# Attention and two MLP layers on one core: four copies per head for six, P x V with one group per column half, another order of work

## The chip, the cores and the metric

The kernel runs on one core of one Trainium2 chip. The metric is device microseconds of one execution. Five engines run side by side, each through its own instructions in order: PE (TensorE, matmul), DVE (VectorE), ACT (ScalarE), POOL (GpSimd) and SP (SyncE, which issues nearly all DMA transfers).

## The reference

Two batches of eight heads, sequence 768, head dimension 64, float32. Each query and each key gets a six-bit bucket from the signs of its projection; a query attends only to keys of its own bucket. The attention output goes through two MLP layers of width 512, 2048, 512.

```python
q_bits = (np.einsum('bhsd,dk->bhsk', q, proj) > 0)      # k_bits the same
mask = q_bucket[:, :, :, None] == k_bucket[:, :, None, :]
scores = np.where(mask, 0.125 * np.matmul(q, k.transpose(0, 1, 3, 2)), -1e9)
attn = softmax(scores)
x = np.matmul(attn, v)                   # to (1536, 512)
h = x @ moe_w_in; x = (P(h) / Q(h)) @ moe_w_out          # rational function
h = x @ moe2_w_in; out = (h * clip(h + 3, 0, 6) / 6) @ moe2_w_out
```

## The kernel before

**Precision.** Products whose operands are split are done as sums of products of a high part (rounded to the matmul format fp32r) and a low part (the rest). A high part is written by ACT or POOL, a low part by DVE or POOL.

**Attention.** The work is 16 heads of three groups, 48 groups in all; a group is 256 query rows in two row blocks of 128. For each head, PE transposes Q and K together (`tp_mm`, L220), ACT copies the result out (`tp_full`), `tp_hi` (TH) and `tp_lo` (TL) make the tiles `th` and `tl`: rows 0 to 63 are Q, rows 64 to 127 are K. The score matmul needs Q and K parts on other partitions, in four tiles: `q1` (q high over q low), `k1` (k high twice), `q2` (q high, then 12 rows of bits) and `k2` (k low, then 12 rows of bits). DMA copies on SP fill them: `spread_hi` (SPH, L244) issues four copies out of `th`, `spread_lo` (SPL, L250) two out of `tl`, `spread_bits` (SB, L270) four small ones out of the bucket bits. Each of the four tiles has two buffers, so the copies of a head wait until the score matmuls of the head two before it are done.

For each group: scores (`s_mm`, S: L342 with `q1` and `k1`, L345 with `q2` and `k2`), row maximum on DVE (L349), exponential on ACT, normalisation on POOL (L370), transposes of P on PE (`p_mm`, L378), copies of them out of PSUM on ACT or DVE (`p_copy`, L388), then P x V (`v_mm`, L396). P x V is done for two groups at a time. Within a group the two row blocks go to the two column halves of the array, 128 columns each, with one PSUM tile `o` per group; `v_out` empties each tile by two copies, the first on ACT, the second on DVE (L409) behind it. PSUM tiles with the tag `T` (transposes, bits, P, `o`) share four buffers.

**Weights.** In the same time the weights of the MLP are loaded (`conv_load`, raw, L102) and split by ACT, DVE and POOL (`conv_a`, `conv_r`, `conv_s`, L119, `conv_add`, `conv_hi`, `conv_lo`). 13 of the 32 tiles of the first layer are ranked by a list `CVS`, the others by their due step and `AHEAD`.

**Layers.** 96 steps follow (2 layers, 3 token blocks, 16 hidden blocks), each of 24 matmuls of 512 columns: 12 into `h` (`in_mm`, L448) and 12 into `acc` (`out_mm`, L516), with the function between them on ACT, DVE and POOL.

**Order.** Everything after `start()` is a list of tasks with engines, rank, dependencies and the buffers they take. `ordered()` walks a model of the engines: whenever an engine is free it takes the ready task of lowest rank. Durations are in `W`, delays to a dependent in `W_LAG` and `LAG`, ranks come from `OFF`, `W_SLOT` per group, `CVS` and `AHEAD`. The instructions are emitted in that order and every engine keeps it, whatever the real durations are. SP is modelled as one engine that is held for a whole transfer.

Of the kernel before, what the change touches and what calls it, by code (L numbers as in the profile page):

```python
# [24 lines left out]
KP = D + 2 * NB  # L25
# [3 lines left out]
CVS = (1, 6, 11, 13, 14, 20, 25, 28, 28, 34, 36, 48, 55)  # L29
RING = {"raw": 3, "cvd": 3, "t1": 2, "t2": 3, "t3": 2, "t4": 1, "gh": 2, "gl": 2}  # L30

W = {"S": 0.70, "M": 0.87, "E": 0.89, "NV": 0.53, "A": 0.28, "N": 0.97, "P": 0.44, "H": 0.485, "H_D": 0.60, "V": 2.85, "OC": 0.23,
     "VA": 0.25, "XH": 0.35, "XL": 0.71, "TP": 0.33, "TF": 0.47, "TH": 0.74, "TH_P": 0.98, "TL": 0.86, "TL_P": 1.95, "Z": 0.85, "ZB": 0.59, 
# [3 lines left out]
     "ld": 2.0, "LQ": 1.6, "LV": 0.9, "SPH": 3.1, "SPL": 1.6, "SB": 1.3, "cf": 1.0}  # L37
W_LAG = {"PE": 0.25, "DVE": 0.13, "ACT": 0.16, "POOL": 0.09, "SP": 2.5, "NONE": 0.0}
LAG = {"A": 0.30, "E": 0.26, "ld": 3.0, "LQ": 2.8}
TLP = 0  # L40
W_SLOT = 5.091

OFF = {"S": -7.496, "rr": -1.217, "M": 7.071, "E": -43.196, "NV": -36.242, "A": 8.173, "N": -5.796, "P": 12.751, "H": 2.136, "V": -12.378, "OC":
       -30.545, "VA": -24.667, "XH": 7.594, "XL": 6.524, "TP": 14.245, "Z": 9.031, "c": -4.166, "SPH": 8.232, "SPL": -22.569, "SB": -11.64, "LQ": -19.047,
       "LV": -42.52, "ld": -12.092, "cf": 7.164}
AHEAD = 0.2557
# [4 lines left out]
def body(tc, q, k, v, proj, moe_w_in, moe_w_out, moe_a, moe_b, moe2_w_in, moe2_w_out, out):  # L51
# [89 lines left out]
    nat, tf, hl, lr, live = {}, {}, {}, {}, {}  # L141
# [15 lines left out]

    zfill = ate.tile([128, 512], F32R, name="zfill")
# [53 lines left out]
    thr = cpool.tile([128, 4], F32, name="thr")  # L212
    zw = ate.tile([128, 32], F32, name="zw")
# [14 lines left out]
    def tp_hi(hd, eng):  # L228
        hl[hd] = tuple(ate.tile([128, S], F32R, name=f"t{x}", tag=f"t{x}{hd % 2}") for x in "hl")
        if eng == "POOL":  # L230
            nc.gpsimd.tensor_scalar(out=hl[hd][0], in0=tf[hd], scalar1=1.0, scalar2=0.0, op0=ALU.mult, op1=ALU.add)
        else:
            act(hl[hd][0], tf[hd])
# [5 lines left out]
    def spread_hi(hd):  # L239
        th = f(hl[hd][0])  # L240
        t = lr[hd] = [ate.tile([128, S], F32R, name=x, tag=x, bufs=2) for x in ("q1", "q2", "k1", "k2")]
        q1, q2, k1, k2 = (f(x) for x in t)
        for dst, src in ((q1[0:64], th[0:64]), (k1[0:64], th[64:128]), (k1[64:128], th[64:128]), (q2[0:64], th[0:64])):
            nc.sync.dma_start(out=dst, in_=src)  # L244

    def spread_lo(hd):
        tl = f(hl[hd][1])
        q1, q2, k1, k2 = (f(x) for x in lr[hd])
        for dst, src in ((q1[64:128], tl[0:64]), (k2[0:64], tl[64:128])):
            nc.sync.dma_start(out=dst, in_=src)  # L250
# [15 lines left out]
    def spread_bits(hd):  # L266
        for i in range(2):
            for n in range(2):
                o = 64 * (hd % 2) + 32 * n + 2 * NB * i
                nc.sync.dma_start(out=f(lr[hd][2 * i + 1])[64:KP, n * 384:(n + 1) * 384], in_=f(live["bt"])[o:o + 2 * NB])  # L270

# [12 lines left out]
    def start():  # L284

        th, tl = hl[0] = tuple(ate.tile([128, S], F32R, name=f"t{x}", tag=f"t{x}0") for x in "hl")
        q1, q2, k1, k2 = lr[0] = [ate.tile([128, S], F32R, name=x, tag=x, bufs=2) for x in ("q1", "q2", "k1", "k2")]

        for n in range(2):
            tp_mm(0, n)  # L290
            c = slice(n * 384, (n + 1) * 384)
            ps = live.pop(("tp", 0, n))
            act(th[:, c], ps, scale=qsc)
            stt(tl[:, c], ps, qsc, f(th)[:, c], ALU.mult, ALU.subtract)
            for dst, t in ((k1[0:64], th), (k1[64:128], th), (k2[0:64], tl)):
                nc.gpsimd.tensor_scalar(out=dst[:, c], in0=f(t)[64:128, c], scalar1=1.0, scalar2=0.0, op0=ALU.mult, op1=ALU.add)
        load_qk(2)
        load_v(0)
        load_v(1)
# [4 lines left out]
        act(q2[0:64], th[0:64])  # L304
# [9 lines left out]
        nc.vector.tensor_copy(out=k2[64:KP], in_=f(bt)[32:32 + 2 * NB])  # L314
        nc.vector.tensor_copy(out=q2[64:KP], in_=f(bt)[0:2 * NB])
# [19 lines left out]
    def s_mm(g, rr):  # L335
        hd, rg = divmod(g, 3)
        q1, q2, k1, k2 = lr[hd]
        r = 2 * rg + rr
        rs = slice(r * 128, (r + 1) * 128)
        ps = sps[(g, rr)] = psc.tile([128, 2, 512], F32, name="s", tag="S", bufs=2)  # L340
        for n in range(2):
            nc.tensor.matmul(out=ps[:, n, 0:384], lhsT=q1[:, rs], rhs=k1[:, n * 384:(n + 1) * 384],  # L342
                             start=True, stop=False)
        for n in range(2):
            nc.tensor.matmul(out=ps[:, n, 0:384], lhsT=q2[0:KP, rs], rhs=k2[0:KP, n * 384:(n + 1) * 384],  # L345
                             start=False, stop=True)
# [43 lines left out]
    def v_mm(g):  # L390
        vs = nat[("v", g // 3)]
        o = live[("o", g)] = psum.tile([128, 128], F32, name="o", tag="T", bufs=4)
        for kt in range(R):
            pt = pts[(g, kt // 2)]
            for rr in range(2):
                nc.tensor.matmul(out=o[64 * rr:64 * rr + 64], lhsT=vs[:, kt], rhs=pt[:, kt % 2, rr * 128:rr * 128 + 128],  # L396
                                 start=(kt == 0), stop=(kt == R - 1))
        for i in range(3):
            pts.pop((g, i))

    def v_out(g, rr):
        main = slice(64 * (g // 3 % 2), 64 * (g // 3 % 2) + 64)
        if rr == 0 and (g // 3) % 2 == 0:
            xts[g % 3] = atl.tile([128, 256], F32, name="xt", tag=f"xt{g % 3}")
        dst, src = xts[g % 3][main, rr * 128:rr * 128 + 128], live[("o", g)][64 * rr:64 * rr + 64]
        if rr == 0:
            act(dst, src)
        else:
            nc.vector.tensor_copy(out=dst, in_=src)  # L409
            live.pop(("o", g))  # L410
# [128 lines left out]
    def add(name, engines, rank, deps, fn, port=(), earliest=0.0, takes=(), frees=()):  # L539


        work[name] = (engines if isinstance(engines, dict) else dict([engines]), rank, [d for d in deps if d in work],
                      fn, port, earliest, takes, frees)

    def plan_attention():
# [3 lines left out]
        def pair(pr):  # L549
# [3 lines left out]
            for hd in heads:  # L553
                if hd > 2:
                    add(("LQ", hd), ("SP", W["LQ"]), (g0 - 9 + 2 * (hd % 2)) * T + OFF["LQ"], [("TP", hd - 2, 1)], lambda e, hd=hd: load_qk(hd))
                for n in range(2):
                    r = (g0 - 9 + 2 * (hd % 2) + n) * T + OFF["TP"]
# [5 lines left out]
                add(("TH", hd), {"ACT": W["TH"], "POOL": W["TH_P"]}, r + 1.2, [("TF", hd, 0), ("TF", hd, 1), ("SPH", hd - 2), ("SPL", hd - 2)],  # L563
                    lambda e, hd=hd: tp_hi(hd, e), pool)
                add(("TL", hd), {"DVE": W["TL"], "POOL": W["TL_P"]}, r + 1.8, [("TH", hd)], lambda e, hd=hd: tp_lo(hd, e), ("POOL", "DVE"))
            r = (g0 - 5) * T + OFF["Z"]
# [4 lines left out]
            for hd in heads:  # L571
                r = (g0 - 4 + 3 * (hd % 2)) * T
                old = [("S", 3 * (hd - 2) + 2, 1)]
                add(("SPH", hd), ("SP", W["SPH"]), r + OFF["SPH"], [("TH", hd)] + old, lambda e, hd=hd: spread_hi(hd))
                add(("SPL", hd), ("SP", W["SPL"]), r + OFF["SPL"], [("TL", hd), ("SPH", hd)], lambda e, hd=hd: spread_lo(hd))
                add(("SB", hd), ("SP", W["SB"]), r + OFF["SB"], [("ZB", pr), ("SPH", hd)], lambda e, hd=hd: spread_bits(hd))

        def vals(hd):
            if hd > 1:
                add(("LV", hd), ("SP", W["LV"]), (3 * hd - 3) * T + OFF["LV"], [("V", 3 * hd - 4 + (hd % 2 == 0))], lambda e: load_v(hd))  # L580

        def group(g):
            hd = g // 3
            b = g * T
            odd, last = hd % 2, g >= NG - 5
            for rr in range(2):
                add(("S", g, rr), ("PE", W["S"]), b + OFF["S"] + OFF["rr"] * rr, [("SB", hd), ("SPL", hd)], lambda e, rr=rr: s_mm(g, rr), takes=("S",),
                    earliest=1.0)
                add(("M", g, rr), ("DVE", W["M"]), b + OFF["M"] + OFF["rr"] * rr, [("S", g, rr), ("N", g - 4, 1)], lambda e, rr=rr: s_max(g, rr))
                add(("E", g, rr), ("ACT", W["E"]), b + OFF["E"] + OFF["rr"] * rr, [("M", g, rr)], lambda e, rr=rr: s_exp(g, rr), takes=("p",),  # L590
# [10 lines left out]
            if g % 2:  # L601
                two = (g - 1, g)
                add(("V", g), ("PE", W["V"]), b + OFF["V"], [("H", x, i) for x in two for i in range(3)] + [("LV", hd), ("LV", (g - 1) // 3)],
                    lambda e: [v_mm(x) for x in two], takes=("T", "T"), frees=tuple(("H", x, i) for x in two for i in range(3)))
                for x in two:
                    add(("OC", x), ("ACT", W["OC"]), b + OFF["OC"], [("V", g), ("XL", x - 3)], lambda e, x=x: v_out(x, 0))
                    add(("VA", x), ("DVE", W["VA"]), b + OFF["VA"], [("OC", x), ("XL", x - 3)], lambda e, x=x: v_out(x, 1),
                        frees=(("V", g),) if x == g else ())
                    if x // 3 % 2:
                        add(("XH", x), {"POOL": W["XH"], "ACT": W["XH"]} if last else ("POOL", W["XH"]), b + OFF["XH"], [("VA", x)],  # L610
# [131 lines left out]
    def ordered():  # L742
# [14 lines left out]
        free, port, held, out, now = {}, 0.0, None, [], 0.0  # L757
# [99 lines left out]
```

## Time and profile before

| | |
|---|---|
| Time, median of 3 runs | 773.3 us (771.25 to 944.34) |
| Time of the profiled execution | 774.28 us |
| Its span, first to last instruction | 772.5 us |
| PE busy | 756.2 us (98%) |
| DVE, ACT, POOL busy | 537.3, 478.8, 384.0 us (70, 62, 50%) |
| DMA | 65.76 MB |

A profile row names a line, an engine, an operation, output<-input, and a count. Busy time of PE counts overlapping matmuls once, and ends of matmuls are modelled; start times are the surer reading. An fp32 matmul that is no transpose shows as two records. In the profile text, "idle before" names what released the engine.

### The profile page before, as it was taken

To read this page: it belongs to the slowest core of one execution; us is meant where nothing else is said; L and a number is where in the kernel's file an instruction comes from. 1 tells how busy PE (TensorE), PEld (TensorE's weight loads), DVE (VectorE), ACT (ScalarE), POOL (GpSimd) and SP (SyncE) were. 2 spreads that over 40 slices of the span, in tenths; PEclk is the share of its full clock that TensorE was granted. 3 is DMA by queue.
4 is the path that set the end of the run, shared out by engine and by line. 5 is a ranking of instruction groups with operands and counts; after the bars stand their busy time and mean duration, and the time that the engine had idled before them with its cause. 6 is when DMAs were issued, how large, how long until landed. Compare 5 with 4: busy or idle time off the path is not lost.

```text
span 772.5 us, 12661 instructions
## 1 busy us (share of the span) xinstructions
PE 756.2 (98%) x4603; PEld 641.1 (83%) x4603; DVE 537.3 (70%) x905; ACT 478.8 (62%) x890; POOL 384.0 (50%) x446
## 2 busy tenths in 40 slices
PE   7989999999999999999999999999999999999998
PEld 6879989888898888888888888888888888888886
DVE  6867989878788999999889999987522322232222
ACT  6878888788567788876558889877422222222221
POOL 6878999979678667722224667877400000000000
PEclk9999999999999999999999999999999999999999
DMA  7785766675331133300002033345100100010001
GB/s 192 190 225 152 181 186 174 155 191 160 104 87 39 71 110 110 109 1 1 0 1 82 5 105 120 113 142 178 49 1 1 55 1 1 0 55 1 0 1 54
DMA packets 47485, 65.76 MB, mean 85 GB/s; under 512 B 29168, under 2 KB 31936, under 8 KB 47424
## 3 DMA queue, kind: packets, MB, share of 16 engines
q1 hardware_dynamic: 46640, 64.76, 29.5%
q8 instruction: 36, 0.59, 0.3%
q10 hardware_dynamic: 784, 0.20, 0.1%
q14 instruction: 25, 0.20, 0.1%
HBM read 43.00 MB, written 3.15 MB: 60 GB/s over the span
## 4 chain that ended last, share of the span: by engine, by line
PE 84%; DMA 6%; ACT 3%; DVE 3%; POOL 1%; issue 1%; SPq 1%; ACTq 0%; POOLq 0%; DVEq 0%
PE acc L516 34%; PE h L448 33%; PE o L396 5%; PE tt L378 5%; PE s L342 3%; PE s L345 3%; DMA raw<-in_moe_w_out_dram 1%; ACT p L55 1%; DMA raw<-in_moe_w_in_dram 1%; DMA k<-th 1%; DMA nv<-in_v_dram 1%; DVE stat L349 1%; SPq L270 1%; DVE t L58 1%; POOL p L370 1%
## 5 line engine op out<-in xcount | busy, mean ns | idle before, releaser
L55 ACT ACTIVATE t<-h,cbias 128x512 f32<-128x512 f32 x48 | 33.0, 689 | 122.9 <-PE h L448 122.9
L505 POOL TENSOR_TENSOR gl<-t,gh 128x512 fp32r<-128x512 f32 x48 | 62.9, 1310 | 92.6 <-ACT gh L55 89.1
L370 POOL TENSOR_SCALAR p<-p,stat 128x768 f32<-128x768 f32 x96 | 100.5, 1055 | 15.5 <-DVE stat L366 7.3
L58 DVE SCALAR_TENSOR_TENSOR t<-t,h 128x512 f32<-128x512 f32 x48 | 33.1, 689 | 108.0 <-ACT t L55 108.0
L123 POOL TENSOR_TENSOR cvd<-cvd,raw 128x512 int32<-128x512 int32 x64 | 87.8, 1376 | 36.0 <-DVE cvd L119 20.7
L349 DVE TENSOR_REDUCE stat<-s 128x1 f32<-128x768 f32 x96 | 88.4, 949 | 8.2 <-PE s L345 7.5
L55 ACT ACTIVATE p<-s,stat 128x768 f32<-128x768 f32 x96 | 85.9, 903 | 12.3 <-DVE stat L349 10.4
L55 ACT ACTIVATE gh<-t 128x512 fp32r<-128x512 f32 x96 | 60.6, 632 | 50.7 <-PE acc L516 42.0
L378 PE MATMUL tt<-ident,p 128*128 128x128 f32 x576 | 71.8, 276 | 2.3 <-ACT pt L55 2.3
L505 DVE TENSOR_TENSOR gl<-t,gh 128x512 fp32r<-128x512 f32 x48 | 37.5, 782 | 51.0 <-PE acc L516 47.5
L58 DVE SCALAR_TENSOR_TENSOR t<-t,coef,h 128x512 f32<-128x512 f32 x96 | 71.4, 744 | 1.7
L378 PEld LDWEIGHTS tt<-ident,p 128*128 128x128 f32 x576 | 66.1, 142 | 6.6 <-ACT pt L55 1.7
L58 DVE SCALAR_TENSOR_TENSOR t<-t,r 128x512 f32<-128x512 f32 x96 | 65.9, 687 | 5.6 <-ACT r L55 2.6
L396 PE MATMUL o<-pt,nv 128*64 128x128 f32 x1152 | 68.6, 275 | 1.0 <-ACT tf L55 1.0
L396 PEld LDWEIGHTS o<-pt,nv 128*64 128x64 f32 x1152 | 62.4, 137 | 8.0 <-issue 4.3
L342 PE MATMUL s<-k,q 128*128 128x384 f32 x192 | 56.0, 372 | 3.2 <-ACT p L55 3.1
L388 DVE COPY pt<-tt 128x512 f32<-128x512 f32 x81 | 51.6, 682 | 4.6 <-PE tt L378 4.0
L516 PE MATMUL acc<-gh,wo_0h 128*128 128x512 f32 x192 | 54.2, 389 | 0.0
L516 PE MATMUL acc<-gh,wo_0l 128*128 128x512 f32 x192 | 54.2, 389 | 0.0
L516 PE MATMUL acc<-gl,wo_0h 128*128 128x512 f32 x192 | 54.2, 389 | 0.0
L516 PE MATMUL acc<-wo_0h,gh 128*128 128x512 f32 x192 | 54.2, 389 | 0.0
L516 PE MATMUL acc<-wo_0l,gh 128*128 128x512 f32 x192 | 54.2, 389 | 0.0
(139 smaller groups left out, 1809.0 us busy)
## 6 DMA issues: line engine op xcount, KB each, us to landing
raw<-in_moe_w_in_dram SPq DMA_DIRECT2D x32, 512.0 KB
raw<-in_moe_w_out_dram SPq DMA_DIRECT2D x32, 512.0 KB
q<-th SPq DMA_DIRECT2D x30, 192.0 KB
k<-th SPq DMA_DIRECT2D x30, 192.0 KB
nqk<-in_q_dram SPq DMA_DIRECT2D x16, 192.0 KB
nv<-in_v_dram SPq DMA_DIRECT2D x16, 192.0 KB
out_dram<-o SPq DMA_DIRECT2D x12, 256.0 KB
nqk<-in_k_dram SPq DMA_DIRECT2D x15, 192.0 KB
```

The source lines that it names most:

```text
L55: nc.scalar.activation(out=out, in_=in_, func=func, **kw)
L58: nc.vector.scalar_tensor_tensor(out=out, in0=in0, scalar=scalar, in1=in1, op0=op0, op1=op1)
L123: nc.gpsimd.tensor_tensor(out=d.bitcast(I32), in0=d.bitcast(I32), in1=raw[:, :, 0], op=ALU.add)
L342: nc.tensor.matmul(out=ps[:, n, 0:384], lhsT=q1[:, rs], rhs=k1[:, n * 384:(n + 1) * 384], start=True, stop=False)
L349: nc.vector.tensor_reduce(out=stats[g % 4][:, rr, 0:1], in_=sps[(g, rr)][:, :, 0:384], axis=AX.XY, op=ALU.max, negate=True)
L370: nc.gpsimd.tensor_scalar(out=pt, in0=pt, scalar1=st[:, rr, 4:5], scalar2=st[:, rr, 5:6], op0=ALU.mult, op1=ALU.add)
L378: nc.tensor.transpose(ps[:, kt, rr], ptile[(g, rr)][:, c:c + 128], ident)
L388: nc.vector.tensor_copy(out=pt, in_=live.pop(("p", g, i)))
L396: nc.tensor.matmul(out=o[64 * rr:64 * rr + 64], lhsT=vs[:, kt], rhs=pt[:, kt % 2, rr * 128:rr * 128 + 128], start=(kt == 0), stop=(kt == R ...
L448: nc.tensor.matmul(out=ps, lhsT=w[:, ws], rhs=x[:, cols(m)], start=(n == 0), stop=(n == 3 * KD - 1))
L505: (nc.gpsimd if eng == "POOL" else nc.vector).tensor_tensor(out=e["gl"], in0=e["2"], in1=f(e["gh"]), op=ALU.subtract)
L516: nc.tensor.matmul(out=acc["o"][i], lhsT=lhsT, rhs=rhs, start=(t == 0 and n == 0), stop=(t == NF - 1 and n == 2))
```

## The change

**K parts in place.** `th`, `tl`, `q1`, `q2` get three buffers each; `k1` and `k2` no longer exist except for head 0. `spread_q` (SPH) copies q high to `q1[0:64]` and to `q2[64:128]`; `spread_k` (SPK) copies k high over the q half of `th`, so that `th` is what `k1` was; `spread_lo` copies q low to `q1[64:128]`; k low stays in `tl[64:128]`, and the bits go over the first 12 rows of `tl` and of `q2`. Rows 12 to 63 of `q2` are zeroed once. So SPK waits for SPH and TL, and the bits of a head wait for its SPH and SPL. The second score matmul contracts over 128 rows instead of 76.

**P x V.** One PSUM tile of 128x256 for the pair: group g-1 in the lower column half, group g in the upper one, 256 columns per matmul. `v_out` is one copy per group, on ACT or DVE.

**Order.** Each DMA task becomes an issue on SP and a transfer on a modelled engine "DMA". `W`, lags, ranks, `CVS`, `W_SLOT` and `AHEAD` have new values; the first two V loads leave `start()` and become ranked tasks. `FREE0` sets when engines are first free.

```diff
-CVS = (1, 6, 11, 13, 14, 20, 25, 28, 28, 34, 36, 48, 55)
+CVS = (-4, 12, 12, 12, 15, 21, 27, 28, 30, 33, 35, 54, 57)
...
-     "ld": 2.0, "LQ": 1.6, "LV": 0.9, "SPH": 3.1, "SPL": 1.6, "SB": 1.3, "cf": 1.0}
-W_LAG = {"PE": 0.25, "DVE": 0.13, "ACT": 0.16, "POOL": 0.09, "SP": 2.5, "NONE": 0.0}
+     "ld": 1.65, "LQ": 1.75, "LV": 0.6, "SPH": 1.55, "SPK": 0.78, "SPL": 0.78, "SB": 0.25, "cf": 0.1}
+ISSUE = {"ld": (0.4, 0), "LQ": (0.65, 0.65), "LV": (0.65, 0), "SPH": (0.6, 0.6), "SPK": (0.6, 0), "SPL": (0.6, 0), "SB": (0.8, 2.3), "cf": (1.0, 0)}
+W_LAG = {"PE": 0.25, "DVE": 0.13, "ACT": 0.16, "POOL": 0.09, "SP": 0.4, "DMA": 1.0, "NONE": 0.0}
...
-W_SLOT = 5.091
+W_SLOT = 4.6575
...
-AHEAD = 0.2557
+AHEAD = -5.5176
...
+    ths, tls, q1s, q2s = ([ate.tile([128, S], F32R, name=f"{x}{i}") for i in range(3)] for x in ("th", "tl", "q1_", "q2_"))
...
+    def spread_q(hd):
+        for dst in (q1s[hd % 3][0:64], q2s[hd % 3][64:128]):
+            nc.sync.dma_start(out=f(dst), in_=f(hl[hd][0])[0:64])
+
+    def spread_k(hd):
         th = f(hl[hd][0])
-        t = lr[hd] = [ate.tile([128, S], F32R, name=x, tag=x, bufs=2) for x in ("q1", "q2", "k1", "k2")]
...
-        for dst, src in ((q1[0:64], th[0:64]), (k1[0:64], th[64:128]), (k1[64:128], th[64:128]), (q2[0:64], th[0:64])):
-            nc.sync.dma_start(out=dst, in_=src)
+        nc.sync.dma_start(out=th[0:64], in_=th[64:128])
 
     def spread_lo(hd):
-        tl = f(hl[hd][1])
-        q1, q2, k1, k2 = (f(x) for x in lr[hd])
-        for dst, src in ((q1[64:128], tl[0:64]), (k2[0:64], tl[64:128])):
-            nc.sync.dma_start(out=dst, in_=src)
+        nc.sync.dma_start(out=f(q1s[hd % 3])[64:128], in_=f(hl[hd][1])[0:64])
...
-            for dst, t in ((k1[0:64], th), (k1[64:128], th), (k2[0:64], tl)):
-                nc.gpsimd.tensor_scalar(out=dst[:, c], in0=f(t)[64:128, c], scalar1=1.0, scalar2=0.0, op0=ALU.mult, op1=ALU.add)
+            for dst in (k1[0:64], k1[64:128]):
+                nc.gpsimd.tensor_scalar(out=dst[:, c], in0=f(th)[64:128, c], scalar1=1.0, scalar2=0.0, op0=ALU.mult, op1=ALU.add)
         load_qk(2)
-        load_v(0)
-        load_v(1)
...
-        nc.vector.tensor_copy(out=k2[64:KP], in_=f(bt)[32:32 + 2 * NB])
-        nc.vector.tensor_copy(out=q2[64:KP], in_=f(bt)[0:2 * NB])
+        nc.gpsimd.tensor_scalar(out=tl[0:2 * NB], in0=f(bt)[32:32 + 2 * NB], scalar1=1.0, scalar2=0.0, op0=ALU.mult, op1=ALU.add)
+        nc.vector.tensor_copy(out=q2[0:2 * NB], in_=f(bt)[0:2 * NB])
...
-            nc.tensor.matmul(out=ps[:, n, 0:384], lhsT=q2[0:KP, rs], rhs=k2[0:KP, n * 384:(n + 1) * 384],
+            nc.tensor.matmul(out=ps[:, n, 0:384], lhsT=q2[:, rs], rhs=k2[:, n * 384:(n + 1) * 384],
                              start=False, stop=True)
...
     def v_mm(g):
-        vs = nat[("v", g // 3)]
-        o = live[("o", g)] = psum.tile([128, 128], F32, name="o", tag="T", bufs=4)
+        o = live[("o", g)] = psum.tile([128, 256], F32, name="o", tag="T", bufs=4)
         for kt in range(R):
-            pt = pts[(g, kt // 2)]
-            for rr in range(2):
-                nc.tensor.matmul(out=o[64 * rr:64 * rr + 64], lhsT=vs[:, kt], rhs=pt[:, kt % 2, rr * 128:rr * 128 + 128],
+            for c, x in enumerate((g - 1, g)):
+                nc.tensor.matmul(out=o[64 * c:64 * c + 64], lhsT=nat[("v", x // 3)][:, kt], rhs=pts[(x, kt // 2)][:, kt % 2],
                                  start=(kt == 0), stop=(kt == R - 1))
...
-        if rr == 0:
+        if eng == "ACT":
             act(dst, src)
         else:
             nc.vector.tensor_copy(out=dst, in_=src)
...
-                add(("TH", hd), {"ACT": W["TH"], "POOL": W["TH_P"]}, r + 1.2, [("TF", hd, 0), ("TF", hd, 1), ("SPH", hd - 2), ("SPL", hd - 2)],
+                add(("TH", hd), {"ACT": W["TH"], "POOL": W["TH_P"]}, r + 1.2 + (OFF["T1H"] if pr == 1 else 0 if pr else OFF["T0H"]), [("TF", hd, 0), ("TF", hd, 1), ("S", 3 * (hd - 3) + 2, 1), ("S", 3 * (hd - 3) + 2, 0)],
...
-                old = [("S", 3 * (hd - 2) + 2, 1)]
-                add(("SPH", hd), ("SP", W["SPH"]), r + OFF["SPH"], [("TH", hd)] + old, lambda e, hd=hd: spread_hi(hd))
-                add(("SPL", hd), ("SP", W["SPL"]), r + OFF["SPL"], [("TL", hd), ("SPH", hd)], lambda e, hd=hd: spread_lo(hd))
-                add(("SB", hd), ("SP", W["SB"]), r + OFF["SB"], [("ZB", pr), ("SPH", hd)], lambda e, hd=hd: spread_bits(hd))
+                old = [("S", 3 * (hd - 3) + 2, 1), ("S", 3 * (hd - 3) + 2, 0)]
+                add(("SPH", hd), ("SP", W["SPH"]), r + OFF["SPH"], [("TH", hd)] + old, lambda e, hd=hd: spread_q(hd))
+                add(("SPL", hd), ("SP", W["SPL"]), r + OFF["SPL"], [("TL", hd)] + old, lambda e, hd=hd: spread_lo(hd))
+                add(("SPK", hd), ("SP", W["SPK"]), r + OFF["SPK"], [("SPH", hd), ("TL", hd)], lambda e, hd=hd: spread_k(hd))
+                add(("SB", hd), ("SP", W["SB"]), r + OFF["SB"], [("ZB", pr), ("SPH", hd), ("SPL", hd)], lambda e, hd=hd: spread_bits(hd))
```

## Rows read from the trace of the kernel before

**Rows 1.** Stretches (start:end, length): busy us of each engine, PE clock, DMA share, GB/s

```profile
64.00:142.00 78.00, 77.84 (x782) 71.05 (x782) 68.98 (x129) 65.66 (x142) 72.53 (x99) 1.00 0.66 179
...
300.00:400.00 100.00, 100.00 (x442) 82.78 (x442) 92.27 (x138) 67.52 (x115) 39.33 (x31) 1.00 0.11 37
```

**Rows 2.** PE in order of time: start, us, engine, line, operation, [idle before <-releaser]

```profile
9.08 0.59 PE L342 MATMUL s<-k,q 128*128 128x384 f32 x2
...
69.73 2.84 PE L396 MATMUL o<-pt,nv 128*64 128x128 f32 x48
...
142.78 2.84 PE L396 MATMUL o<-pt,nv 128*64 128x128 f32 x48
...
240.04 0.50 PE L448 MATMUL h<-xh,wi_0h 128*128 128x512 f32 x1
...
249.79 2.84 PE L396 MATMUL o<-pt,nv 128*64 128x128 f32 x48
252.56 0.50 PE L448 MATMUL h<-xh,wi_0h 128*128 128x512 f32 x1
```

**Rows 3.** PE's waits, 0 to 260 us: waiter <- releaser: total, times, longest

```profile
PE s L342 <- ACT p L55: 3.1, 3, 2.3
PE tt L378 <- ACT pt L55: 2.3, 2, 1.5
PE tp L220 <- DMA nqk<-in_k_dram: 2.3, 2, 1.2
...
PE tp L220 <- DVE pt L388: 1.2, 2, 1.0
PE o L396 <- ACT tf L55: 1.0, 2, 0.5
PE s L345 <- DVE q L315: 0.6, 1, 0.6
```

**Rows 4.** All engines in order of time around the longest wait and two later ones

```profile
48.09 0.66 ACT L55 ACTIVATE cvd<-raw 128x512 f32<-128x512 f32 x1 [3.64 <-DMA raw<-in_moe_w_in_dram]
...
50.69 0.62 PE L342 MATMUL s<-k,q 128*128 128x384 f32 x2 [2.34 <-ACT p L55]
...
52.39 2.70 PE L378 MATMUL tt<-ident,p 128*128 128x128 f32 x12
...
101.26 1.48 PE L378 MATMUL tt<-ident,p 128*128 128x128 f32 x12
...
147.83 0.68 ACT L55 ACTIVATE cvd<-raw 128x512 f32<-128x512 f32 x1 [1.80 <-DMA raw<-in_moe_w_out_dram]
...
180.06 0.50 DVE L409 COPY xt<-o 64x128 f32<-64x128 f32 x2 [2.19 <-ACT xt L55]
...
208.85 0.66 ACT L55 ACTIVATE raw<-raw 128x512 int32<-128x512 uint32 x1 [3.25 <-DMA raw<-in_moe_w_in_dram]
```

**Rows 5.** Stretch of the slow clock, columns as in the first group

```profile
52.00:54.00 2.00, 2.00 (x12) 1.97 (x11) 1.39 (x4) 1.95 (x6) 1.67 (x1) 0.61 1.11 223
```

**Rows 6.** SP's own waits, 10 to 240 us, columns as for PE

```profile
SPq L244 <- PE s L342: 36.9, 10, 8.0
```

**Rows 7.** DMA issues on SP: ns min/median/max of one issue

```profile
L244 SPq DMA_DIRECT2D q<-th x30: 473/540/1296, 10.9 to 213.5; - x30
...
L270 SPq DMA_DIRECT2D q<-bt x30: 757/784/1262, 15.5 to 217.1; - x30
```

**Rows 8.** Chain of waits: start, us, what

```profile
11.50 7.09 DMA k<-th
...
58.19 2.24 DMA q<-bt
```

**Rows 9.** Instructions that touch xt, ns min/median/max, and who waited for it (us, times)

```profile
L55 ACT ACTIVATE xt<-o x48: 254/269/278, 30.7 to 254.5; 64x128 f32<-64x128 f32 x48
L409 DVE COPY xt<-o x48: 285/293/295, 31.0 to 255.3; 64x128 f32<-64x128 f32 x48
...
DVE xt L409: 15.4, 22
```

## What the change is expected to do

> **What bounds the kernel now.** I read the stretches first, then PE in order of time, then who waited for whom, then SP's queue. The layers come first because they are the larger part: in 100 us of them PE starts 442 matmuls of 512 columns, one every 226 ns, and is never idle [rows 1]. Nothing in that part can be made shorter by this change; 96 steps of 24 such matmuls are 521 us. So the question is when the attention lets go of PE.
>
> PE's rows give the pace there. Between the P x V of the pair at 69.73 and that at 142.78 lie eight pairs, 16 groups, in 73.05 us: 4.57 us per group [rows 2]. In that stretch PE is busy 77.84 of 78 us, with POOL at 72.5 and DVE at 69.0 close behind [rows 1]. That is the pace of a full PE. The whole attention takes longer: its first score matmul starts at 9.08 and its last P x V gives way at 252.56, 243.5 us, of which 30 matmuls of the first layer (those that start between 240.04 and 249.79) are 30 x 0.226 = 6.8. 236.7 us remain for 48 groups, and 48 x 4.57 = 219.4. So 17.3 us are lost outside the full pace [rows 1, 2]. The 98% of the page hides them, since a short wait is partly covered by the modelled end of the matmul before it.
>
> The waits name most of the 17.3: 3.1 for exponentials, 2.3 for copies of P on ACT, 2.3 for K loads, 1.2 for copies on DVE, 1.0 for ACT's `tf`, 0.6 for the bits of head 0, 10.5 in all [rows 3]. Behind the longest (2.34 at 50.69) the granted clock falls to 0.61 in the mean of two microseconds [rows 5], between the levels 2.4 and 1.2 GHz, after PE had stood still; twelve transposes take 2.70 us there and 1.48 elsewhere, 1.2 more [rows 4]. That makes 11.7. The other 5.6 are the ramp of the first groups and small change.
>
> Why are exponentials and copies late? ACT works in order, and it stood 3.64, 1.80 and 3.25 us before a weight tile whose load had not landed [rows 4]. The work behind it is what PE wants. The loads were late because SP issues in order and stood 36.9 us, up to 8.0 at a time, before `spread_hi`, for the score matmuls of the head two before [rows 6]. So the root is SP's queue.
>
> **The change, part by part.**
>
> *P x V.* Before, 48 records of 128 columns take 252.56 - 249.79 = 2.77 us, 57.7 ns each, and 24 pairs do this [rows 2]. After, 24 records of 256. If a column costs what it does now, nothing changes: 0. If a column takes one clock of 2.4 GHz, 128 take 53.3 ns; if the other 4.4 are paid per record, a pair takes 24 x (106.7 + 4.4) = 2.67, 0.10 less, 2.4 in all. The nearest row of longer streams, 512 columns in 226 ns [rows 1], is 0.442 ns per column, so 24 x 256 x 0.442 = 2.715, 0.055 less. I take that: 24 x 0.055 = 1.3 us. Loss I exclude: both halves of the array already run with weights and moving data of their own, since 128 columns of a two-record product would otherwise not pass at this rate.
>
> The Trainium skill (TensorEngine Tiling (Array Packing), Instruction Overhead) gives each matmul about 60 cycles of overhead, by which halving their number would be worth 12 x 25 ns = 0.3 us per pair, an estimate from that page; the sum below would come out about 6 us lower. The row of 57.7 ns for 128 columns does not agree with it [rows 2].
>
> *Emptying `o`.* 48 copies on ACT (269 ns) and 48 on DVE (293 ns), each of the latter behind one on ACT, become 48 of double width on whichever is free [rows 9]. Engine time falls from 27.0 us to 48 times something between 0.29 (width costs nothing) and 0.59 (double), so it moves between 13 down and 1 up; it is not on PE's path. What matters: DVE stood 15.4 us in 22 waits behind ACT [rows 9], one of them, 2.19 us at 180.06 [rows 4], ahead of the late DVE copy that PE waited 1.2 for [rows 3]. A pair also takes one `T` buffer instead of two, and the second half of P x V no longer waits for one: 1.0 in two waits [rows 3]. Together 2.2, between 0 and 2.2.
>
> *Copies of K.* Six large issues per head become four. At 0.54 to 0.6 us each [rows 7] SP saves 1.2 us per head and the queues 2 x 192 KB x 15 = 5.9 MB. More weighs the third buffer: the copies of a head wait for the head three before, so they have 27 us (two heads at 3 x 4.57) instead of 14, and the 36.9 us of standing go. What waited for late data then goes: the 2.34 for exponentials [rows 4], 2.3 for copies on ACT and 2.3 for K [rows 3], and the 1.2 of slow clock, 8.1 us; between 0 (loads late for another reason) and 8.1. I take all of it, since each of these is a wait for a load or stands behind an ACT that stood for one. The other 0.8 of the exponentials I leave.
>
> *New waits on SP.* `spread_k` waits for the reads of `spread_q`, the bits for the low part to have landed. Behind them in SP's queue stand weight, Q, K and V loads. A large copy took up to 7.09 us in the crowded start, bits 2.24 [rows 8]: 9.3 us in the worst case, within the 27. I cost the wait itself at nothing for that reason, and without that cover the loads are late as before and the 8.1 just claimed stay. The second score matmul over 128 rows instead of 76 streams the same 384 columns: 0.
>
> *Start.* The low K copies on POOL fall away, and DVE writes the bits of Q without those of K before them: the 0.6 wait goes [rows 3], I count 0.5. V loads move behind the first weights; P x V needs them only after scores, exponentials and transposes of two groups: nothing.
>
> *The new order* is new everywhere, and an order from a model leaves waits where the model errs. Without the longest, the old one left 11 waits of (10.5 - 2.34) / 11 = 0.74 us in the mean [rows 3]. I charge two of them, +1.5; ends 0 and the 8.2 of all.
>
> Sum: -1.3 - 2.2 - 8.1 - 0.5 + 1.5 = -10.6. The profiled execution took 774.3, 1.0 more than the median of 773.3; 774.3 - 10.6 = 763.7, so 762.7 beside the median.
>
> **The rivals.**
>
> *Everything clean (0.22).* All waits go, no new ones, and some 4 of the 5.6 us of ramp too, because loads no longer crowd it: 774.3 - 1.3 - 11.7 - 4 = 757.3, 756 beside the median. For it speaks the stretch that already runs at full pace; against it POOL at 93% there.
>
> *SP stands elsewhere (0.14).* The new waits hold SP as the old ones did, loads are late as before: -1.3 - 2.2 - 0.5 leaves 770.3, 769. For it: 8.0 us of standing happened with one wait per head [rows 6]. Against it: the third buffer. The Trainium skill says (DMA: Bandwidth & Descriptors, Anatomy of one DMA) that a DMA engine does not wait for semaphores and the wait is the issuing sequencer's; the 36.9 us on SP agree [rows 6].
>
> *Given back behind the attention (0.09).* An attention 11 us shorter leaves weights unconverted that were done within it. In the layers DVE is busy 92.3 of 100 us [rows 1]; `AHEAD` ranks conversions later still. If PE waits for weights by what it won, 773. Against it: 7.7 us free per 100 there.
>
> *Slower (0.05).* The chain of copies of a head, now with two steps more in series, lands after its first score matmul wants it. Each time costs the longest wait and its clock, 2.34 + 1.2 = 3.5 us [rows 3 to 5]. From eight of 15 heads on it decides: 762.7 + 8 x 3.5 = 791. It needs chains over 27 us where the rows show 9.3.
>
> **How the numbers follow.** My forecast has 0.50, with 758 to 768 as its own range. With the clean case below it and the two cases that give the gain back above, 754 to 772 leaves out about 2 in 10. 2% is about what a measurement of this kernel can tell from no change: faster than 757.8 or slower than 788.8. Faster: the clean case and the forecast's edge, 0.24. Slower: 0.05. Same: 0.71.
>
> **What would show it.** P x V of a pair lasting 2.70 to 2.73 us, 24 records; first score matmul of the layers at 228 to 231 instead of 240; no wait of SP for L342's matmuls; ACT without stands of over 1 us before raw tiles; granted clock 1.00 through 64 us. It is wrong if PE waits over 6 us between 20 and 240, if SP stands for long before the bits or `spread_k`, or if PE waits in the layers at all.

## The result, and the profile after

The changed kernel takes 780.4 us in the median, the kernel before 773.5 us in the same comparison; the ratio is 1.0074, 95% interval 1.0046 to 1.0102. It is slower by 0.7%, where 762.7 us had been forecast and 754 to 772 given as the range. One odd execution, 2530 us with every matmul some three times as long, fell on its profile, so the lines here are from the same kernel run again (`a0_after`: 780.42 us, 1.0068 [1.0041, 1.0095]), whose profiled execution took 775.23 us with a span of 773.4.

> The changed kernel as it is, for a trace of it in its usual speed (the profiled execution that came with it took 2530 us, every matmul over three times as long). Time near 780 us. Theory of the clock: its mean granted clock is 0.991 to 0.993 where the kernel before has 0.998, so over its span of 777 us about 777 x 0.008 / 0.5 = 12 us were run at 1.2 GHz instead of 3; the trace should show two to four stretches at half clock, each behind a wait of PE of about 2 us or more, all within the first 260 us, and the layers at 442 matmuls per 100 us as before. Theory of the layers: PE waits for weights between 250 and 400 us, since AHEAD ranks the conversions later; then the window 300 to 400 us shows fewer than 430 matmuls. Theory of SP: SP stands for over 20 us in all before the bits or the copy of K.

PE in order of time in `a0_after`; columns as in [rows 2]:

```profile
9.21 0.59 PE L346 MATMUL s<-k,q 128*128 128x384 f32 x2
...
24.92 0.59 PE L346 MATMUL s<-th,q 128*128 128x384 f32 x2 [3.97 <-issue]
28.65 0.98 PE L349 MATMUL s<-tl,q 128*128 128x384 f32 x2 [3.14 <-DMA q<-bt]
...
34.39 1.47 PE L382 MATMUL tt<-ident,p 128*128 128x128 f32 x12
...
36.83 1.15 PE L225 MATMUL tp<-ident,nqk 128*128 128x128 f32 x9
38.21 2.81 PE L398 MATMUL o<-pt,nv 128*64 128x256 f32 x24 [0.23 <-DVE pt L392]
...
251.09 2.81 PE L398 MATMUL o<-pt,nv 128*64 128x256 f32 x24
253.83 0.50 PE L450 MATMUL h<-xh,wi_0h 128*128 128x512 f32 x1
```

The same view of the kernel before has its first P x V here:

```profile
27.19 2.84 PE L396 MATMUL o<-pt,nv 128*64 128x128 f32 x48
```

These rows, with [rows 2], hold the result as far as this execution shows it. It is the shortest of its ten: its span is 0.9 us longer than before, while the medians lie 5 to 7 us apart. From the first P x V to the start of the last one takes 212.9 us (251.09 - 38.21) where it took 222.6 (249.79 - 27.19): 9.7 us won. But from the first scores to the first P x V, the ramp, takes 29.0 us (38.21 - 9.21) where it took 18.1 (27.19 - 9.08): 10.9 lost. The last P x V gives way at 253.83 instead of 252.56.

Not all of either number is waiting. The new order does 36 transposes of P and 24 of Q and K before its first P x V, the old one 24 and 15; the 12 at 34.39 and the nine at 36.83 are work that the old order has in the steady part. They take about 2.3 us, an estimate from their rows (1.22 to the next start, and some 1.1). So about 8.6 us are lost in the ramp and 7.4 are won behind it.

The stretches of both kernels show the same without a choice of marks; columns as in [rows 1]. First before, then `a0_after`:

```profile
9.00:24.00 15.00, 12.50 (x76) 9.17 (x75) 11.75 (x22) 12.15 (x24) 11.79 (x15) 1.00 0.87 213
24.00:40.00 16.00, 16.00 (x173) 14.95 (x170) 13.01 (x25) 14.07 (x32) 14.21 (x20) 1.00 0.80 197
40.00:64.00 24.00, 20.99 (x197) 18.01 (x196) 15.25 (x31) 19.02 (x42) 19.39 (x27) 0.93 0.77 203
...
142.00:220.00 78.00, 73.24 (x748) 65.74 (x748) 61.38 (x117) 55.41 (x121) 62.76 (x89) 1.00 0.58 151
```

```profile
9.00:24.00 15.00, 10.30 (x60) 7.78 (x58) 12.04 (x19) 13.48 (x27) 10.96 (x13) 1.00 1.13 263
24.00:40.00 16.00, 11.71 (x78) 8.79 (x80) 8.84 (x18) 8.08 (x18) 7.08 (x11) 0.79 0.58 133
40.00:64.00 24.00, 23.93 (x179) 19.07 (x176) 21.42 (x40) 19.07 (x39) 21.24 (x31) 1.00 0.68 171
64.00:142.00 78.00, 77.30 (x587) 61.43 (x586) 67.37 (x123) 60.86 (x125) 71.66 (x99) 1.00 0.50 129
142.00:220.00 78.00, 75.59 (x579) 60.35 (x577) 66.43 (x120) 56.98 (x116) 66.58 (x93) 1.00 0.54 138
...
300.00:400.00 100.00, 100.00 (x443) 82.81 (x442) 92.75 (x138) 65.46 (x111) 38.70 (x31) 1.00 0.09 30
```

Of `a0_after` in shorter stretches:

```profile
28.00:32.00 4.00, 3.35 (x13) 1.71 (x14) 1.83 (x4) 0.99 (x2) 0.93 (x1) 0.50 0.91 198
32.00:36.00 4.00, 4.00 (x32) 3.87 (x31) 3.32 (x8) 2.99 (x7) 1.46 (x4) 0.94 0.55 117
```

From 40 to 220 us PE stands 0.07, 0.70 and 2.41 us where it stood 3.01, 0.16 [rows 1] and 4.76, and the clock of 0.93 is 1.00. From 9 to 40 it stands 2.20 us more, then 4.29 where it stood nothing, and behind that the granted clock is 0.79 in the mean of 16 us (0.50, the 1.2 GHz level, between 28 and 32). PE worked in only part of that time, so the clock cost about 1.9 us of columns (half of 3.35, and 0.06 of 4.00). Together that is 8.4 us, nearly all of the 8.6. The layers run as in [rows 1]. Of the three theories put down for this run the first came nearest, with one stretch at half clock instead of two to four.

Why head 1 is late is in SP's queue. First SP of `a0_after`, then of the kernel before, in order of time (start, us, line, tile<-source, count):

```profile
13.17 0.59 SPq L150 DMA_DIRECT2D nqk<-in_q_dram  x1
13.80 0.67 SPq L150 DMA_DIRECT2D nqk<-in_k_dram  x1
14.57 0.60 SPq L253 DMA_DIRECT2D q<-tl  x1
15.21 1.07 SPq L104 DMA_DIRECT2D raw<-in_moe_w_in_dram  x2
16.87 0.51 SPq L250 DMA_DIRECT2D th<-th  x1
17.43 0.60 SPq L150 DMA_DIRECT2D nqk<-in_q_dram  x1
18.07 0.76 SPq L150 DMA_DIRECT2D nqk<-in_k_dram  x1
18.93 1.34 SPq L104 DMA_DIRECT2D raw<-in_moe_w_in_dram  x1
20.32 0.43 SPq L323 DMA_DIRECT2D coef<-in_moe_a_dram  x1
20.80 0.43 SPq L324 DMA_DIRECT2D coef<-in_moe_b_dram  x1
21.33 3.98 SPq L274 DMA_DIRECT2D q<-bt  x2
```

```profile
15.49 2.20 SPq L270 DMA_DIRECT2D q<-bt  x2
```

The new order puts nine issues that head 1 doesn't need ahead of its bits: Q and K of two heads (0.59 + 0.67 + 0.60 + 0.76), three weight tiles (1.07 + 1.34) and the coefficients (0.86), 5.9 us together. 21.33 - 5.9 is 15.4, where the bits stood before; what moving these issues gives in fact, the experiments show. The bits are also slow: the DMA share is 1.13 in that stretch where it was 0.87, and the chain of waits of `a0_after` has 6.86 us for them, against 2.24 for a later head in [rows 8]:

```profile
21.33 6.86 DMA q<-bt
```

The bits make the second of PE's two stops, 3.14 us. The first, 3.97 us before 24.92, comes ahead of the half of head 1's scores that reads `th` and `q1` and no bits; the profile names no releaser for it. The last copy that this half needs is `spread_k`, issued at 16.87, 8.05 us earlier. `c1_oldv` below, with the same list on SP, has 7.91 us there (18.62 to 26.53). Where the three weight loads come behind, it is 4.02 in `a2_bits` (17.84 to 21.86) and 4.81 in `a4_late1` (18.84 to 23.65). So these loads probably delay copies that are issued already, and not only the issues behind them.

PE's waits from 40 to 256 us in `a0_after`, columns as in [rows 3]; no others are left:

```profile
PE tt L382 <- ACT pt L57: 1.2, 1, 1.2
PE s L349 <- DMA tl<-bt: 1.1, 2, 0.8
PE s L346 <- ACT p L57: 0.5, 1, 0.5
```

SP's own wait for the copies of K in `a0_after`, which took the place of [rows 6]:

```profile
SPq L250 <- DMA q<-th: 9.1, 7, 4.8
```

### The profile page after: what moved, and what is told of

The parts are those of the page before. It is cut to its first block, busy times and chain, and to the rows that moved or that the text cites. A ratio compares the mean times of both kernels' runs of the same rounds, so it can differ in the third digit from the quotient of the medians.

```text
span 2528.2 us, 11364 instructions
## 1 busy us (share of the span) xinstructions
PE 2523.2 (100%) x4027; PEld 1352.4 (53%) x4027; DVE 546.7 (22%) x896; ACT 484.8 (19%) x862; POOL 372.0 (15%) x436
## 4 chain that ended last, share of the span: by engine, by line
PE 100%; ACT 0%; DVE 0%; issue 0%
PE h L450 34%; PE acc L518 34%; PE o L398 9%; PE tt L382 9%; PE s L346 5%; PE s L349 5%; PE tp L225 2%; PE z L260 1%; PE warm L286 0%; PE warm L200 0%; PE z L315 0%; PE pst L306 0%; ACT o L57 0%; DVE zfill L162 0%
## 5 line engine op out<-in xcount | busy, mean ns | idle before, releaser
L382 PE MATMUL tt<-ident,p 128*128 128x128 f32 x576 | 244.5, 688 | 0.0
L398 PE MATMUL o<-pt,nv 128*64 128x256 f32 x576 | 238.9, 1089 | 0.0
L518 PE MATMUL acc<-gh,wo_0l 128*128 128x512 f32 x192 | 175.9, 1096 | 0.0
L518 PE MATMUL acc<-gh,wo_0h 128*128 128x512 f32 x192 | 175.7, 1096 | 0.0
L518 PE MATMUL acc<-gl,wo_0h 128*128 128x512 f32 x192 | 175.1, 1094 | 0.0
L518 PE MATMUL acc<-wo_0l,gh 128*128 128x512 f32 x192 | 147.0, 928 | 0.0
L518 PE MATMUL acc<-wo_0h,gh 128*128 128x512 f32 x192 | 147.0, 928 | 0.0
L518 PE MATMUL acc<-wo_0h,gl 128*128 128x512 f32 x192 | 145.9, 923 | 0.0
L349 PE MATMUL s<-tl,q 128*128 128x384 f32 x192 | 144.1, 893 | 0.0
L346 PE MATMUL s<-th,q 128*128 128x384 f32 x180 | 142.1, 915 | 0.0
```

The costliest lines, as they stand in the source:

```text
L349: nc.tensor.matmul(out=ps[:, n, 0:384], lhsT=q2[:, rs], rhs=k2[:, n * 384:(n + 1) * 384], start=False, stop=True)
L382: nc.tensor.transpose(ps[:, kt, rr], ptile[(g, rr)][:, c:c + 128], ident)
L398: nc.tensor.matmul(out=o[64 * c:64 * c + 64], lhsT=nat[("v", x // 3)][:, kt], rhs=pts[(x, kt // 2)][:, kt % 2], start=(kt == 0), stop=(kt ...
L518: nc.tensor.matmul(out=acc["o"][i], lhsT=lhsT, rhs=rhs, start=(t == 0 and n == 0), stop=(t == NF - 1 and n == 2))
```

## The experiments

All in one table; the ramp is from the first scores to the first P x V, the steady part from there to the start of the last P x V, both of the profiled execution. In the kernels of the new order (a and c) the ramp holds the 2.3 us of transposes that the others have in the steady part.

| kernel | us | ratio to before, 95% | ramp | steady |
|---|---|---|---|---|
| before | 773.5 | | 18.1 | 222.6 |
| a0_after | 780.4 | 1.0068 [1.0041, 1.0095] | 29.0 | 212.9 |
| a1_loads | 774.9 | 1.0008 [0.9986, 1.0031] | 23.4 | 214.6 |
| a2_bits | 778.9 | 1.0074 [1.0044, 1.0104] | 31.0 | 213.9 |
| a4_late1 | 777.5 | 1.0029 [1.0008, 1.0051] | 28.3 | 216.5 |
| a5_late3 | 776.6 | 1.0020 [0.9996, 1.0044] | 21.9 | 218.2 |
| b1_v | 774.3 | 0.9991 [0.9968, 1.0015] | 19.7 | 222.2 |
| c1_oldv | 779.0 | 1.0062 [1.0043, 1.0082] | 28.5 | 212.9 |
| b2_k | 777.5 | 1.0037 [1.0015, 1.0059] | 17.7 | 221.0 |
| b3_vk | 776.05 | 1.0016 [0.9995, 1.0036] | 20.7 | 221.2 |
| b2c_k | 783.9 | 1.0123 [1.0098, 1.0148] | 18.8 | 230.9 |
| b3c_vk | 783.0 | 1.0107 [1.0076, 1.0138] | 18.2 | 230.9 |

**Weights behind head 1.** `a1_loads` changes SP's list alone.

```diff
     todo = ordered()
+    late = [x for x in todo if x[1] in (("is", "ld", 1), ("is", "ld", 2), ("is", "ld", 3))]
+    todo = [x for x in todo if x not in late]
+    at = [x[1] for x in todo].index(("is2", "SB", 1)) + 1
+    todo[at:at] = late
```

> The changed kernel with one move in SP's list: the loads of weight tiles 1, 2 and 3 (3 x 512 KB), issued at 15.2 to 18.9 us ahead of the bits of head 1, come right behind those bits. The order elsewhere is the changed kernel's. Theory of the order: PE's stand before head 1's scores (24.9 and 28.7 us, 7.1 us of idle and some 4 us at half clock behind it) came from those loads in front; the bits land near 20 instead of 28 us, the stand falls under 2 us, and the time falls by 6 to 9 us to 771 to 774. Theory of the chain: the bits are late because they wait in series for the low part to land and `spread_k` for `spread_q`; then the stand stays over 5 us and the time at 778 or more.

The ratio is 1.0008 instead of 1.0068, 0.6% or some 4.6 us less, and the two intervals do not meet. So three weight loads ahead of head 1's bits cost most of what the change lost. Where it went is less sure. The profiled ramp is 23.4 instead of 29.0 us, and the steady part gave 1.7 back; but the first scores of this execution came at 12.51, so that its span is only 0.6 us shorter, and `a4_late1` below, with the same loads behind the bits and first scores at 9.32, has a ramp of 28.3. A late start alone doesn't shorten the ramp: `c1_oldv`, with the loads ahead, started at 11.78 and has 28.5.

**The rest behind it too.** `a2_bits` moves the loads of Q and K of heads 4 and 5 and of the coefficients as well.

```diff
+    later = [("is", "LQ", 4), ("is2", "LQ", 4), ("is", "LQ", 5), ("is2", "LQ", 5), ("is", "ld", 1), ("is", "ld", 2), ("is", "ld", 3), ("is", "cf")]
...
```

> The changed kernel with SP's list in the ramp put so that after the Q copies of head 1 come its low part, its k copy and its bits, and only then the loads of heads 4 and 5, the weight tiles 1 to 3 and the coefficients (with the weights alone moved, the k bits of head 1 still landed 3.1 us after PE wanted them, and a half-clock stretch followed). Theory of the order: the bits land before PE wants them, from the first score matmul to the first P x V it takes 18 to 20 us as in the kernel before instead of 29 (23.4 with the weights alone moved), and the time is 768 to 772. Theory of the chain: the serial waits alone make head 1 late; the first P x V stays 22 us or more behind the first scores, and the time at 774 or more.

A miss: the ramp is 31.0. All engines of `a2_bits` in order of time:

```profile
21.86 0.62 PE L346 MATMUL s<-th,q 128*128 128x384 f32 x2 [0.92 <-DMA th<-th]
...
31.35 0.66 ACT L57 ACTIVATE cvd<-raw 128x512 f32<-128x512 f32 x1 [7.81 <-DMA raw<-in_moe_w_in_dram]
...
32.95 1.01 PE L346 MATMUL s<-th,q 128*128 128x384 f32 x2 [4.48 <-ACT p L57]
```

and its SP between 12 and 26 us:

```profile
12.89 0.46 SPq L253 DMA_DIRECT2D q<-tl  x1
17.84 0.46 SPq L250 DMA_DIRECT2D th<-th  x1
18.39 2.38 SPq L274 DMA_DIRECT2D q<-bt  x2
...
25.17 2.05 SPq L104 DMA_DIRECT2D raw<-in_moe_w_in_dram  x3
```

The bits go out 2.9 us earlier, at 18.39, and PE stands only 0.92 us for head 1's copy of K. But SP stands 4.5 us (12.89 + 0.46 to 17.84) before `spread_k`, with nothing behind it being issued. The weights then go out at 25.17, and ACT, whose order still has their conversion early, stands 7.81 us for the first. PE waits 4.48 behind ACT. The wait had only changed its engine.

**ACT's order as well.** `a4_late1` is `a1_loads` with the conversion of the three tiles 6 us later in the planned order; `a5_late3` moves Q and K of head 5 and the coefficients behind the bits too.

```diff
+    conv = [(n, j) for n in ("ca", "cr") for j in (1, 2, 3)] + [("sh", 1), ("sh", 2), ("add", 1), ("hi", 1), ("lo", 1)]
+    todo = sorted(todo, key=lambda x: x[0] + (6.0 if x[1] in conv else 0.0))
...
```

> The changed kernel with the loads of weight tiles 1 to 3 behind head 1's bits, as in a1_loads, and in addition the work on those three tiles that ACT, DVE and POOL do (11 steps of their conversion) 6 us later in the planned order. a1_loads took 774.85 us and ACT stood 3.1 us there for the first late tile. Theory 'the ramp is paid because weights and head 1 compete, on SP and then on ACT': with ACT no longer asking early the time from first scores to first P x V, 23.4 us in a1_loads, falls to 20 to 22 and the kernel takes 770 to 773. Rival 'the chain of head 1's copies alone makes the ramp': it stays at 23 to 24 and the kernel at 774 to 776.

> As a4_late1, and the loads of Q and K of head 5 and of the coefficients, four issues that still stand ahead of head 1's bits on SP (2.5 us of it there in a1_loads), are put behind them too; head 4's Q and K stay ahead of the waits of spread_k. Theory: bits land 2 to 2.5 us earlier than in a4_late1, the ramp is 18 to 20 us and the kernel takes 766 to 770, faster than both kernels. Rival 'the bits wait for spread_q's landing and not for SP': SP stands in the place of the issues, the ramp is as in a4_late1 and the time within 1 us of it.

Half a miss. The ramp of `a5_late3` came down to 21.9, but its steady part grew to 218.2, and the time stayed at 776.6. PE in order of time in `a5_late3`:

```profile
43.90 0.58 PE L346 MATMUL s<-th,q 128*128 128x384 f32 x2 [2.74 <-issue]
...
45.93 3.95 PE L398 MATMUL o<-pt,nv 128*64 128x256 f32 x24
```

A stop of 2.74 us before head 2's first scores, at 43.9, takes part of it back, and the P x V behind it takes 3.95 us. The profile names no releaser; SP issued head 2's `spread_k` at 41.15 there and at 38.26 in `a0_after`, so the issues put behind head 1 probably hold up the next head. In `a4_late1` the profiled ramp did not shrink (28.3); in that execution SP issued `spread_k` 4.1 us after `spread_lo` (14.78 to 18.84), in `a1_loads` 0.7 us after it. Neither kernel is faster than `a1_loads` (1.0029 and 1.0020 against 1.0008), and what makes the rest of the ramp's loss is not settled by these runs.

**P x V alone, and everything but P x V.** `b1_v` has the new P x V in the order of before; `c1_oldv` the old P x V, two tiles and two copies per group, in the new order.

```diff
+        o = live[("o", g)] = psum.tile([128, 256], F32, name="o", tag="T", bufs=4)
...
+            for c, x in enumerate((g - 1, g)):
+                nc.tensor.matmul(out=o[64 * c:64 * c + 64], lhsT=nat[("v", x // 3)][:, kt], rhs=pts[(x, kt // 2)][:, kt % 2],
...
```

> The kernel before, in its own order of tasks, with P x V done the new way alone: 256 columns per matmul, one group per column half, one PSUM tile per pair; of a pair's two copies out, the first is on ACT and the second on DVE, each where a copy stood. Expected: a pair takes 2.74 instead of 2.77 us as in the trace of the changed kernel, 0.7 us in 24 pairs; the waits of the second half of P x V for a PSUM buffer (1.0 us in two) go, and DVE's 15 us of waits behind ACT's copy of `o` shrink to under 8. In all 1 to 3 us less than before, 772 to 774. Rival: the copies' new places disturb as much as they save; within 0.5 us of before.

> The changed kernel, in its own order, with P x V done the old way: 128 columns per matmul, two PSUM tiles per pair, and each group emptied by two copies on the engine that the order names. What the new P x V is worth in this order. 24 x 0.03 = 0.7 us of PE time, 48 more copies of some 0.28 us on ACT and DVE, and a buffer more taken of the four: 1 to 4 us slower than the changed kernel, 781 to 784. Rival: as in the old order (ratio 0.999) it is worth nothing that can be measured; within 1 us of 780.

0.9991 alone, and 1.0062 without it beside 1.0068 and 1.0074 with it: the P x V is worth nothing that can be measured, in either order.

**K parts alone.** `b2_k` has the K parts and their three buffers in the order of before, `b3_vk` the new P x V as well. Both leave a dependency out: three heads write their parts into buffers that the last scores of three earlier heads have still to read, and some of those scores come out wrong. Their times are therefore those of the same work without that wait. `b2c_k` and `b3c_vk` are the same with the copies of a head moved behind the last scores that read its buffers.

```diff
...
+    for hd in range(4, 16):
+        names = [x[1] for x in todo]
+        last = max(names.index(("S", 3 * hd - 7, r)) for r in range(2))
+        held = [x for x in todo[:last] if x[1] in (("TH", hd), ("TL", hd), ("SPH", hd), ("SPL", hd), ("SB", hd))]
+        todo = [x for x in todo[:last + 1] if x not in held] + held + todo[last + 1:]
```

> The kernel before, in its own order of tasks, with the K parts alone: four large copies per head for six, three buffers, k high copied over q high in place right behind the low part, bits into `tl` and `q2`. Theory of the third buffer: SP's 36.9 us of standing before the spread copies go, loads land earlier, and the waits of ACT before raw tiles (3.6, 1.8, 3.3 us) shrink; 3 to 7 us less than before, 768 to 772. Theory that the loads were late for another reason (the order itself issues them late): under 1 us less. Theory of the serial chain: the first heads' scores are late as in the changed kernel, 5 us or more above before.

> The kernel before, in its own order of tasks, with both parts, P x V and K. If the ramp loss of the changed kernel lies in its order alone, this has the gain of both parts without that loss: 4 to 10 us less than before, 765 to 771. If the loss lies in the copies' chain, it is at 778 or above, as the changed kernel.

> The kernel before, in its own order, with the K parts alone, as the earlier run of this kind, but with high and low part of heads 8, 13 and 15 written only behind the scores of the head that still read their buffers (in the earlier run they were written ahead of them, so that the last score blocks of heads 5, 10 and 12 were computed from wrong parts). Theory of the moved wait: SP's 37 us before the spread copies go, but `spread_k` stands some 40 to 50 us for the reads of `spread_q`, one stand of 2 to 6 us per head; the time is 1 to 4 us above before, 775.5 to 778. Theory of the third buffer: 768 to 772.

> The kernel before, in its own order, with both parts, P x V and K, and the same mending of heads 8, 13 and 15. Parts without the new order: if the steady stretch of the changed kernel (first to last P x V 9.7 us shorter than before) owes its gain to the parts, this is at 765 to 770, since the ramp of the old order stays; if to the new order, it is within 3 us of the kernel before.

SP's own waits in `b2c_k`, then in `b2_k`:

```profile
SPq L252 <- DMA q<-th: 53.8, 15, 5.8
```

```profile
SPq L252 <- DMA q<-th: 48.7, 15, 6.0
```

The ramp of `b2c_k` is as before, 18.8 us. SP stands 53.8 us, 15 times, before `spread_k` for the reads of `spread_q`, where it stood 36.9 for score matmuls [rows 6], and the steady part is 8.3 us longer than before. But the standing doesn't explain that: in `b2_k` it is 48.7 us, and the steady part is 221.0, 1.6 shorter than before (`b3_vk`: 221.2). What `b2c_k` loses against `b2_k` comes with the tasks that were moved by hand; which of them costs it, these runs don't show. What they do show is that the K parts win nothing in the old order, even without the dependency (1.0037). In the new order, which puts other work between the two copies, the same wait is 9.1 us in 7 times and the steady part 212.9. So the K parts with the new order win the steady part, and the new order loses the ramp, where these parts alone lose little. The new order without the K parts was not run.

## Why the prediction was wrong

*What bounds the kernel* held for the steady part. 9.7 us went there, 7.4 without the transposes that moved, where the terms for it sum to 10.1. They came out of waits for exponentials and copies and the slow clock [rows 3 to 5]; PE's waits after 40 us add up to 2.8 us, where they were 8.0. Two of the prediction's own signs speak against the rest of it: PE waits 10.1 us between 20 and 240, over the 6 named, and the first matmul of the layers starts at 239.78 instead of 228 to 231. The rival "given back behind the attention" falls: the layers hold 443 matmuls in 100 us without a gap.

*P x V* (forecast 2.715 us a pair) measured 2.74 (251.09 to 253.83), and was 2.77. So 24 pairs make 0.7 us, half of the 1.3 forecast, and both ways of measuring it alone cannot tell it from nothing. The estimate from the Trainium skill's 60 cycles per matmul (TensorEngine Tiling (Array Packing), Instruction Overhead), 0.3 us per pair, does not agree with the 0.03 measured.

*Emptying `o`.* Double width costs DVE 0.43 and ACT 0.38 us, inside the bounds of 0.29 and 0.59. DVE's stand behind ACT's half went from 15.4 us [rows 9] to 7.6, and 5.5 are new, for PE:

```profile
DVE xt L412 <- ACT xt L57: 7.6, 9, 1.5
DVE xt L412 <- PE o L398: 5.5, 8, 1.5
```

`c1_oldv` has the same steady part without it, so nothing of the 2.2 us claimed shows as this edit's.

*Copies of K*: 8.1 us were claimed for the third buffer. The waits went, but not for that reason alone: `b2_k` and `b2c_k` have that buffer, and SP stands longer than before, 48.7 and 53.8 us, with no gain in time. The rival "SP stands elsewhere" describes the K parts by themselves, in the old order.

*New waits on SP* is the step that failed. They were priced at nothing because a chain of 9.3 us has a cover of 27. That cover belongs to heads that are copied while others are computed. Head 1 has only head 0 before it: its copies have to land within the ramp, all of which was 18.1 us. There PE stood 3.97 and 3.14 us for them. The price was also taken from the copies alone, not from what the new order puts between them on SP: 5.9 us of other issues, and bits that took 6.86 us instead of 2.24. `a1_loads` takes three of the nine away and is 0.6% faster, some 4.6 us.

*Start* was counted as -0.5, with the row of the crowded start, 7.09 us for one copy [rows 8], used only as a bound. The new order puts three weight loads between head 1's copies (15.21 and 18.93), where the old one had none between 8.17 and 22.52, and ACT's order waits for them (7.81 us in `a2_bits`); the clean rival even had "loads no longer crowd it". This term and the new waits fall into the same stretch, and no run parts them: together they stood at -0.5, and the ramp is +10.9, 8.6 without the transposes.

*The new order* got +1.5 for waits in the steady part. There it was worth more than it cost; its errors sat in the ramp, where nothing was ahead to cover them.

With +10.9 in the place of -0.5 and -9.7 for the steady terms, the sum for the profiled execution is 774.3 + 1.2 = 775.5, and it took 775.2; both terms are measured between the same marks, so this is a check of the sum and of no cause. The median lies 5 us above that execution, and these 5 us are the larger part of the loss against the kernel before. The execution's mean clock is 0.995; of the nine others eight have 0.991 to 0.993 and take 778.6 to 784.1. 0.003 of 780 us is 2.3 us of full clock, so about half of the 5 goes with a slower clock; that the rest are longer stops of PE in the ramp, which the slow clock follows in the rows above, is an inference, since no trace shows one of these executions.

The "slower" rival, a chain that lands after its first scores want it, was right in its mechanism for one head, not for eight of 15, and in the ramp, not in the steady part; it had 0.05.

## What to carry to other kernels

Price a chain of waits by the place with the least work ahead of it, not by the mean: the first head has no cover. When an order is new, list what stands on each in-order queue between two steps of that chain in the ramp, DMA issues included, before counting any gain of the steady part. And a load that is moved out of the way is still wanted at its old time by an engine whose order has stayed: ACT stood 7.81 us for one in `a2_bits`.

## What was not expected of the hardware

The issue of two small bits copies, 18 KB each, took SP 3.98 us where the DMA share had been 1.13, and 2.20 before at 0.87 (`a1_loads`: 1.75). The Trainium skill (Perfetto Trace Analysis, DMA Instruction — HWDGE) says that such a row covers a wait for a lock and the making of the descriptors, and not the data's movement; which of the two grew no run here shows.

The first scores started at 9.1 to 9.7 us in seven of the profiled executions of the table and at 11.7 to 12.5 in the other five, in kernels of either order; the ramp is counted from them for that reason.
